# Pooled attention and a top-1 mixture of experts in one kernel: V's columns set in their slots by VectorE products with a mask in PSUM, in place of small DMA copies

## The chip, the cores and the metric

One core of one Trainium2 chip runs the whole kernel. The metric is the device time of one execution in microseconds (us), as the median of several runs.

## What is computed

Eight batches of eight heads, 576 tokens each, 64 wide. Keys and values are averaged over groups of 8 tokens, so that each head has 72 pooled keys. Attention over them gives 4608 tokens of 512 numbers. A gate (512 x 8) sends each token to one of eight experts, and the expert is two matrix products with a relu between.

```python
k_p = k.reshape(B, H, Sp, pool, D).mean(axis=3)
v_p = v.reshape(B, H, Sp, pool, D).mean(axis=3)
scores = scale * np.matmul(q, k_p.transpose(0, 1, 3, 2))
attn = np.exp(scores - np.max(scores, axis=-1, keepdims=True))
attn = attn / (np.sum(attn, axis=-1, keepdims=True) + 1e-09)
x = np.matmul(attn, v_p)
...
logits = x @ w_gate
expert_idx = np.argmax(logits, axis=1)
...
    h = np.maximum(x_sorted[lo:hi] @ w1[e], 0.0)
    y_sorted[lo:hi] = h @ w2[e]
return gate_w[:, None] * y
```

## The kernel before

The order of the work is written out by hand. It has two stages.

**Attention: 36 units.** A unit is 128 tokens of one batch with all eight heads. Batches go in pairs: units 0 to 3 are the first batch of a pair, 4 to 7 the second, and unit 8 takes the last 64 tokens of both; four pairs give 36 units. So batch 2 starts in unit 9, batch 3 in 13, batch 4 in 18, batch 5 in 22, batch 6 in 27 and batch 7 in 31. The loop at L1008 issues for unit i, in this order:

- `u_pt` (L520): TensorE turns the unit's probabilities (`both`) in five pieces of 128 columns into the PSUM tile `pp` (L524); ScalarE copies it to `ph` in fp16 (L526). `pp` has one buffer of 1024 columns, of which 640 are used.
- `g_s` (L485): scores of a later unit into `ps` (L500), `g_qt`: queries turned into `pq` (L477).
- `u_lo` (L529): VectorE makes `pl`, what fp16 lost of `pp` (L532); `g_min` (L507): `nmx`, a minimum over the scores (L510); ScalarE's exponentials follow (L517).
- `u_pv` (L535): 24 products of `ph` and `pl` with the values in `VB` into `po` (L558, in unit 8 of a pair L553). `po` has one buffer.
- `u_nrm` (L575): VectorE reads `po`, takes reciprocals (`ri`, L588, L590) and writes the normalised rows to `both` (L592).

Pieces of other work, "fillers", are put between the steps of `u_nrm` on VectorE: the routing of earlier units to experts (L616 to L755) and the last steps on V.

**The values' slots.** The pooled rows of a batch are 576 (8 heads by 72), cut in five pieces of 128 partitions. A piece holds rows of up to three heads, and a product in L558 takes all of a piece's rows at once; so each head has a slot of its own in `VB` (5 pieces by 3 slots by 78 columns, high and low halves), which holds that head's rows and zeros elsewhere. The finished columns of a batch stand in `vc` (72 columns per piece: 64 of V and 8 of V times the gate). Two ways lead from `vc` to `VB`:

- batches 0 and 1: `masked` (L448), two VectorE products of `vc`, broadcast over the slots, with a 0/1 mask in SBUF (`mk16`), 1080 elements per partition each;
- batches 2 to 7: the last step on V (`low`, L432) puts 12 small DMA copies in the list `moves`, one for each head and piece (8 to 72 partitions of 2 by 72 fp16). SyncE issues them at L1043, at most four at the end of a unit before unit 30 and at most eight after. One copy of a batch's keys within `BD` (L389) goes by the same list.

`VB` has three buffers. That of batches 2 and 5 is used again, after unit 26, for the rows of the first block of tokens (`xg`, L218). `blank` (L284) clears all of this one and sets columns 72 of the others.

SyncE has one queue in program order: it also issues the loads of K, V and queries, the weight loads (L102), the load of the first routed tokens (`early_load`, L929) and the transposes of these (`turn`, L915). What is behind an entry that waits, waits too. GpSimd pools K and V (L327 to L330), sends rows to their experts (L707), and splits the first tokens for the experts (`first_block`, L900, L901). The first products of the experts (`up_early`, L996) stand within units 33 to 35.

**Experts.** From about unit 35 on the kernel runs blocks of 256 tokens through the experts (L989 to L1326).

`prep` (L831) and the lines behind it say in which unit a batch's steps are issued.

Of the kernel before, what the change touches and what calls it, by code (L numbers as in the profile page):

```python
# [13 lines left out]
OP = mybir.AluOpType  # L14
# [18 lines left out]
def kernel(  # L33
# [248 lines left out]
        nc.gpsimd.memset(BD[i], 0.0)  # L282

    def blank(i):  # L284
        nc.gpsimd.memset(VB[i] if i == 2 else VB[i][:, 1, :, :, 72:73], 0.0)
        nc.gpsimd.tensor_tensor(VB[i][:, 0, :, :, 72:73], mk16[:, :, :, None], z16[:, :, :, None], op=OP.add)

    for i in range(3):
# [114 lines left out]
    def five(pm, o, n):  # L403
        return pm[:, o:o + 5 * n].rearrange("p (c x) -> p c x", c=5)
# [12 lines left out]
    def u_dve(b, early=False):  # L417
        pm, vc = KVS["pu", b], KVS["vc", b]
        ut = work.tile([128, 5, 3, E], F32, name="ut", bufs=1)
        u = five(pm, UU, E)  # L420

        def cross():
            nc.vector.tensor_tensor(ut, pm[:, 0:UX].rearrange("p (c s e) -> p c s e", s=3, e=E),
                                    mks[:, :, :, None].to_broadcast([128, 5, 3, E]), op=OP.mult)

        def gather():
            nc.vector.tensor_reduce(u, ut.rearrange("p c s e -> p c e s"), axis=AX.X, op=OP.add)

        def high():
            nc.vector.tensor_scalar(vc[:, 0, :, D:], u, 1.0, None, op0=OP.mult)  # L430

        def low():  # L432
            KVS.pop(("pu", b))
            nc.vector.tensor_tensor(vc[:, 1, :, D:], u, vc[:, 0, :, D:], op=OP.subtract)
            if b > 1:
                KVS.pop(("vc", b))
                for c in range(5):
                    for s in range(*SLOTS[c]):
                        h = HS[c] + s
                        r0, r1 = max(KP * h, 128 * c) - 128 * c, min(KP * h + KP, 128 * c + 128) - 128 * c  # L440
                        moves.append((VB[b % 3][r0:r1, :, c, s, 0:D + E], vc[r0:r1, :, c, :]))

        first = [cross, gather, high, low] if early else [lambda: v_dve(b), cross, gather, high, low]
        if b < 2:
            first += [lambda: masked(b, 0), lambda: masked(b, 1)]
        fillers[0:0] = [(-1, False, f) for f in first]

    def masked(b, s):  # L448
        vc = KVS["vc", b] if s == 0 else KVS.pop(("vc", b))
        nc.vector.tensor_tensor(VB[b][:, s, :, :, 0:D + E], vc[:, s, :, None, :].to_broadcast([128, 5, 3, D + E]),  # L450
                                mk16[:, :, :, None].to_broadcast([128, 5, 3, D + E]), op=OP.mult)

    units = []
    groups = []
# [65 lines left out]
    def u_pt(i):  # L520
        p = pbuf[i % 4]
        pp = psA.tile([128, 1024], F32, name="pp")
        for c in range(5):
            nc.tensor.transpose(pp[:, c * 128:(c + 1) * 128], p[:, c * 128:(c + 1) * 128], ident)  # L524
        ph = work.tile([128, 640], F16, name="ph")
        nc.scalar.activation(ph, pp[:, 0:640], AF.Copy, scale=SP)  # L526
        PP_[i] = (pp, ph)
# [299 lines left out]
    def put(i, pos, f, *a):  # L827
        assert 0 <= i < NU
        hooks.setdefault((i, pos), []).append((f, a))

    def prep(b, k, v, u):  # L831
        put(k[0], "pe" + k[1], k_pe, b)
        put(k[0], "act" + k[1], k_act, b)
        put(v[0], "pe" + v[1], v_pe, b)
        put(v[0], "act" + v[1], v_act, b)
        put(u[0], "pe" + u[1], u_pe, b)
        put(u[0], "act", v_copy, b)
        put(u[0], "dve", u_dve, b)

    put(0, "act2", k_pe, 1)  # L840
    put(0, "act2", k_act, 1)
# [2 lines left out]
    put(2, "pe", u_pe, 1)  # L844
    put(2, "act", v_copy, 1)
    put(2, "dve", u_dve, 1)
    put(1, "sp", load_kv, 3, kf)
    order = [(b, kf if x == 0 else vf) for b in range(B) for x in range(2)]
    for g in range(NPAIR):
# [158 lines left out]
    for i in range(NU):  # L1008
        A, Z = halves.get(2 * i), halves.get(2 * i + 1)
        Y = halves.get(2 * i - 1)  # L1010
        run(i, "q")
        flush(1)
        if i:
            u_pt(i)
        if A:
            g_s(*A)
        if Y:
            g_exp(*Y)
        if i in turns:
            g_qt(*turns[i])  # L1020
        if (i, "pe") not in hooks:
            fill_pe()
        run(i, "pe")
        if i:
            u_lo(i)
        if A:
            g_min(*A)
            fill()
            g_exp(*A)
        fill()  # L1030
        run(i, "act")
        run(i, "dve")
        if i:
            u_pv(i)
        run(i, "pe2")
        if i == 29:
            KVS["late"] = 1
        if len(pend) > 2:
            flush(1)
        fill_pe()  # L1040
        run(i, "sp")
        for _ in range(min(4 if i < 30 else 8, len(moves))):
            nc.sync.dma_start(*moves.pop(0))  # L1043
        if Z:
            g_s(*Z)
        u_nrm(i, (lambda: g_min(*Z)) if Z else None)
        run(i, "act2")
        run(i, "dve2")
        last = routes(i)
        fill(2 if i >= NU - 3 else 1)  # L1050
# [304 lines left out]
```

## Time and profile before

| | us |
|---|---|
| runs | 625.05, 628.80, 632.38 (median 628.80) |
| profiled execution | 626.51 |
| its span, first to last instruction | 623.9 |
| TensorE busy in the span | 574.6 (92%) |
| VectorE, ScalarE, GpSimd busy | 300.7, 291.2, 273.8 |
| mean granted TensorE clock, 1 is full speed | 0.975 |

The profile is one execution on the hardware. PE is TensorE's matmuls, PEld its weight loads, DVE VectorE, ACT ScalarE, POOL GpSimd, SPq the queue of SyncE. "L558" is line 558 of the kernel before. "[1.52 <-DMA vb<-vc]" behind an instruction says that its engine was idle for 1.52 us before it and that the copy from `vc` to `vb` ended that. Tile names are printed in small letters and without the number of the buffer.

### The profile page before, as it was taken

The numbers are of one execution on the slowest core, as the hardware profiler recorded it, in microseconds if no ns is written. First come the engines' busy times: TensorE is split into PE (matmuls) and PEld (weight loads), VectorE is DVE, ScalarE is ACT, GpSimd is POOL, SyncE is SP. The second block draws the span as 40 slices with busy tenths as digits, with TensorE's granted clock in tenths as the row PEclk, the third lists the DMA queues.
The fourth block names the chain that finished last, engine by engine and source line by source line (L and its number), as shares of the span: only waits on it lengthen the run. The fifth ranks groups of instructions, "written<-read, shape, count | busy, mean of one in ns | idle before, by whom it ended". The sixth has DMA issues, their size and how long they took to land.

```text
span 623.9 us, 15851 instructions
## 1 busy us (share of the span) xinstructions
PE 574.6 (92%) x4695; PEld 423.2 (68%) x4696; DVE 300.7 (48%) x613; ACT 291.2 (47%) x648; POOL 273.8 (44%) x524
## 2 busy tenths in 40 slices
PE   6897889799788898998899999999999989999995
PEld 6786779788767375675667667767667666667663
DVE  6567677677667427222782773123722271222122
ACT  2586679789962126223663672122722361222122
POOL 6799588798776543112342223222311232112213
PEclk9799898899979899999999999999999999999998
DMA  8997679879566745974789498343231334321200
GB/s 236 312 294 236 192 223 265 301 233 272 189 203 256 206 128 122 398 203 88 206 279 295 119 310 310 108 105 79 60 73 54 94 75 105 88 49 54 67 17 31
DMA packets 104171, 108.15 MB, mean 173 GB/s; under 512 B 62278, under 2 KB 72518, under 8 KB 104136
## 3 DMA queue, kind: packets, MB, share of 16 engines
q1 hardware_dynamic: 97496, 86.72, 49.3%
q0 software_dynamic: 6640, 20.99, 9.1%
q8 instruction: 19, 0.31, 0.2%
q14 instruction: 16, 0.13, 0.1%
HBM read 72.99 MB, written 23.37 MB: 154 GB/s over the span
## 4 chain that ended last, share of the span: by engine, by line
PE 50%; SPq 1%; issue 1%; ACT 1%; DVE 1%; ACTq 1%; DMA 0%; POOLq 0%; POOL 0%; DVEq 0%
PE po L1073 14%; PE pq L1073 11%; PE ps L998 4%; PE ps L996 4%; PE ps L997 4%; PE pq L996 2%; PE pp L996 2%; PE pp L997 2%; PE pq L997 2%; PE pq L998 2%; PE pp L998 2%; SPq L918 1%; DMA vb<-x_by_expert 0%; ACTq L1212 0%; ACT w L116 0%
## 5 line engine op out<-in xcount | busy, mean ns | idle before, releaser
L1073 PEld LDWEIGHTS <-bd 128*128 128x128 f16 x936 | 91.5, 98 | 109.8 <-issue 5.2
L1242 POOL TENSOR_TENSOR spacer<-ql,iG 1x1 f32<-1x1 f32 x44 | 20.3, 462 | 200.2 <-ACT ql L1238 195.8
L1067 DVE SCALAR_TENSOR_TENSOR bd<-ps,bd 128x512 f16<-128x512 f32 (+1 forms) x44 | 27.6, 630 | 156.8 <-ACT bd L1064 156.2
L517 ACT ACTIVATE both<-ps,nmx 128x72 f32<-128x72 f32 x288 | 68.6, 328 | 14.1 <-DVE nmx L510 13.4
L1073 PE MATMUL po<-w,bd 128*128 128x512 f16 x264 | 58.9, 379 | 0.0
L1073 PE MATMUL po<-kv,bd 128*128 128x512 f16 x264 | 58.8, 379 | 0.0
L1064 ACT ACTIVATE bd<-ps 128x512 f16<-128x512 f32 (+1 forms) x44 | 24.0, 547 | 70.4 <-PE L996 42.2
L1243 POOL DMA_INDIRECT out_dram<-ql,iG x44 | 46.2, 1050 | 21.4 <-issue 20.3
L500 PE MATMUL ps<-bd,qT 128*128 128x144 f32 x256 | 47.9, 314 | 1.7 <-DVE bd L783 0.9
L558 PE MATMUL po<-vb,ph 128*128 128x146 f16 (+2 forms) x384 | 33.2, 233 | 16.4 <-DMA vb<-vc 9.1
L1073 PE MATMUL pq<-kv,bd 128*128 128x512 f16 x216 | 48.1, 379 | 0.0
L1073 PE MATMUL pq<-w,bd 128*128 128x512 f16 x192 | 45.0, 389 | 2.1 <-issue 2.0
L996 PE MATMUL ps<-kv,qt 128*128 128x256 f16 (+1 forms) x176 | 44.9, 263 | 2.1 <-issue 2.1
L998 PE MATMUL ps<-kv,qt 128*128 128x256 f16 (+1 forms) x176 | 44.8, 263 | 2.0 <-DVE qt L118 2.0
L996 PE MATMUL ps<-kv,w 128*128 128x256 f16 (+1 forms) x176 | 43.1, 258 | 2.0 <-ACT kv L116 1.9
L997 PE MATMUL ps<-kv,qt 128*128 128x256 f16 (+1 forms) x176 | 44.9, 263 | 0.0
L998 PE MATMUL ps<-kv,w 128*128 128x256 f16 (+1 forms) x176 | 43.1, 258 | 1.6 <-DVE w L118 1.6
L707 POOL DMA_INDIRECT x_by_expert<-both,rpos x36 | 36.5, 1013 | 15.5 <-issue 6.0
L997 PE MATMUL ps<-kv,w 128*128 128x256 f16 (+1 forms) x176 | 43.1, 258 | 0.0
L1238 ACT ACTIVATE ql<-po,gB 128x512 f32<-128x512 f32 x22 | 15.0, 684 | 57.8 <-PE L996 33.7
L558 PEld LDWEIGHTS <-ph 128*128 128x128 f16 x384 | 26.4, 99 | 21.0 <-DMA vb<-vc 7.9
L996 PEld LDWEIGHTS <-qt 128*128 128x128 f16 x352 | 34.4, 98 | 8.1 <-issue 2.7
(247 smaller groups left out, 1364.7 us busy)
## 6 DMA issues: line engine op xcount, KB each, us to landing
both<-in_moe_w_dram SPq DMA_DIRECT2D x6, 2048.0 KB, 11.4
st<-in_moe_w_dram SPq DMA_DIRECT2D x6, 2048.0 KB, 14.4
vb<-x_by_expert SPq DMA_DIRECT2D x16, 578.0 KB
st<-in_moe_w_dram SPq DMA_DIRECT2D x8, 1024.0 KB
kv<-in_k_dram SPq DMA_DIRECT2D x7, 1024.0 KB
kv<-in_v_dram SPq DMA_DIRECT2D x7, 1024.0 KB
qt<-in_q_dram SPq DMA_DIRECT2D x6, 1024.0 KB
qt<-in_q_dram SPq DMA_DIRECT2D x4, 512.0 KB
```

What stands on the lines that cost most here:

```text
L500: nc.tensor.matmul(ps[:, x * 2 * KP:(x + 1) * 2 * KP], t[:, h, :], BD[b % 3][:, :, h, :], start=True, stop=True)
L517: nc.scalar.activation(p[:, h * KP:(h + 1) * KP], ps[:, x * KP:(x + 1) * KP], AF.Exp, bias=nmx[:, x:x + 1], scale=-1.0)
L558: nc.tensor.matmul(po[:, half, cols], a[:, c * 128:(c + 1) * 128], VB[b % 3][:, y, c, sl, 0:CW], start=st, stop=False, skip_group_check=True)
L707: st = nc.gpsimd.indirect_dma_start(out=xs, out_offset=bass.IndirectOffsetOnAxis(ap=Z["pos"][:, u:u + 1], axis=0), in_=X[:, u, :], in_offs ...
L996: nc.tensor.matmul(dst, wh, xT[:, d, 0:n], start=(d == 0), stop=False)
L997: nc.tensor.matmul(dst, wh, xT[:, DC + d, 0:n], start=False, stop=False)
L998: nc.tensor.matmul(dst, wl, xT[:, d, 0:n], start=False, stop=(d == DC - 1))
L1064: nc.scalar.activation(pair(hT[0], k, n), ups_of(k, n), AF.Relu)
L1067: V.scalar_tensor_tensor(pair(hT[1], k, n), ups_of(k, n), 0.0, pair(hT[0], k, n), op0=OP.max, op1=OP.subtract)
L1073: nc.tensor.matmul(y, hT[x][:, f, 128 * j:128 * j + 128], W2[s][z][:, f, :], start=(half == x == z == f == 0), stop=(half == z == 1 and f ...
L1242: nc.gpsimd.tensor_tensor(spacer[:, 0:1], ys[j][0:1, 0:1], iG[0:1, j:j + 1].bitcast(F32), op=OP.add)
L1243: st = nc.gpsimd.indirect_dma_start(out=out, out_offset=bass.IndirectOffsetOnAxis(ap=iG[:, j:j + 1], axis=0), in_=ys[j], in_offset=None, b ...
```

## The change

`VB` of every batch is now filled by `masked`, and no copy from `vc` to `VB` is left. For batches 1 to 7 the mask is not `mk16` in SBUF but fp32 in 15 of the free columns of `pp`, 640 to 654: in the units named by `put_masked` TensorE multiplies `mk` by the identity into them, right behind the five turns of that unit. The two products of a batch stand before `u_pv` in the program of one unit each (batches 2 to 7: units 6 and 7, 10 and 11, 13 and 14, 19 and 20, 22 and 23, 28 and 29), those of batch 1 both in unit 3. Batch 0 keeps the mask in SBUF. `moves` now holds only the copies within `BD`, and all that stand in the list are issued at the end of each unit. The buffer of batches 2 and 5 is no longer cleared whole.

```diff
     def blank(i):
-        nc.gpsimd.memset(VB[i] if i == 2 else VB[i][:, 1, :, :, 72:73], 0.0)
+        nc.gpsimd.memset(VB[i][:, 1, :, :, 72:73], 0.0)
...
-            if b > 1:
-                KVS.pop(("vc", b))
-                for c in range(5):
-                    for s in range(*SLOTS[c]):
-                        h = HS[c] + s
-                        r0, r1 = max(KP * h, 128 * c) - 128 * c, min(KP * h + KP, 128 * c + 128) - 128 * c
-                        moves.append((VB[b % 3][r0:r1, :, c, s, 0:D + E], vc[r0:r1, :, c, :]))
+            KVS["whole", b] = True
...
-        if b < 2:
+        if b == 0:
             first += [lambda: masked(b, 0), lambda: masked(b, 1)]
...
     def masked(b, s):
+        assert KVS["whole", b]
         vc = KVS["vc", b] if s == 0 else KVS.pop(("vc", b))
-        nc.vector.tensor_tensor(VB[b][:, s, :, :, 0:D + E], vc[:, s, :, None, :].to_broadcast([128, 5, 3, D + E]),
-                                mk16[:, :, :, None].to_broadcast([128, 5, 3, D + E]), op=OP.mult)
+        m = five(KVS["pp"], MK, 3) if b else mk16
+        nc.vector.tensor_tensor(VB[b % 3][:, s, :, :, 0:D + E], vc[:, s, :, None, :].to_broadcast([128, 5, 3, D + E]),
+                                m[:, :, :, None].to_broadcast([128, 5, 3, D + E]), op=OP.mult)
+
+    MK = 640
+    mask_at = set()
...
+        if i in mask_at:
+            KVS["pp"] = pp
+            nc.tensor.matmul(pp[:, MK:MK + 15], ident, mk.rearrange("p c s -> p (c s)"), start=True, stop=True)
...
+    def put_masked(b, *at):
+        for s, i in enumerate(at):
+            mask_at.add(i)
+            put(i, "dve", masked, b, s)
+
...
+        put_masked(b, u[0] + 1, u[0] + 2)
...
+    put_masked(1, 3, 3)
...
-        for _ in range(min(4 if i < 30 else 8, len(moves))):
+        while moves:
             nc.sync.dma_start(*moves.pop(0))
```

**Three places in the order.** In the changed kernel L509, L523, L534, L590, L592 and L594 are L510, L524, L532, L588, L590 and L592 of before.

VectorE in unit 19 before: from the minimum at the end of unit 18 to the normalised rows of unit 19.

```order
L510 TENSOR_REDUCE nmx<-ps 128x4
L532 SCALAR_TENSOR_TENSOR pl<-pp,ph 128x640
L510 TENSOR_REDUCE nmx<-ps 128x4
L715 TENSOR_REDUCE rso<-roh 128x8
L588 TENSOR_SCALAR ri<-po 128x8
L590 RECIPROCAL ri<-ri 128x8
L685 TENSOR_REDUCE res<-rex 128x6
L592 TENSOR_TENSOR both<-po,ri 128x576
```

The same place in the changed kernel; `vb_163` is the buffer of batches 2 and 5.

```order
L509 TENSOR_REDUCE nmx<-ps 128x4
L534 SCALAR_TENSOR_TENSOR pl<-pp,ph 128x640
L509 TENSOR_REDUCE nmx<-ps 128x4
L717 TENSOR_REDUCE rso<-roh 128x8
L446 TENSOR_TENSOR vb_163<-vc,pp 128x15x72
L590 TENSOR_SCALAR ri<-po 128x8
L592 RECIPROCAL ri<-ri 128x8
L687 TENSOR_REDUCE res<-rex 128x6
L594 TENSOR_TENSOR both<-po,ri 128x576
```

Batch 5's first product stands between the minimum and the reading of `po`. It reads `pp`, which unit 20's turns write next.

TensorE at the start of unit 19 in the changed kernel: scores, the five turns, the mask, scores, queries, keys of batch 6.

```order
L499 MATMUL ps<-bd_159,qT 128x144 x2
L523 MATMUL pp<-ident,both 128x128 x5
L526 MATMUL pp<-mk,ident 128x15
L499 MATMUL ps<-bd_160,qT 128x144 x2
L476 MATMUL pq<-ident,qt_155 128x128 x4
L362 MATMUL pq<-ident,kp 64x128 x4
```

The row L526 is new; the others stand as before.

SyncE in units 29 to 31 before: the load of the first routed tokens, the second part of batch 7's copies, the transposes, a weight load.

```order
L929 DMA vb_163<-x_by_expert 128x2x578
L928 UNCONDITIONAL_BRANCH x2
L1043 DMA vb_162<-vc 40x2x72
L1043 DMA vb_162<-vc 32x2x72
L1043 DMA vb_162<-vc 72x2x72
L1043 DMA vb_162<-vc 24x2x72
L1043 DMA vb_162<-vc 48x2x72
L1043 DMA vb_162<-vc 72x2x72
L1043 DMA vb_162<-vc 8x2x72
L1043 DMA vb_162<-vc 64x2x72
L915 DMA_TRANSPOSE kv_130<-bd_160 128x8x128 x2
L102 DMA st_64<-in_moe_w_dram 128x2x1024
```

The same place in the changed kernel, from the last copy within `BD` on.

```order
L1052 DMA bd_159<-bd_159 64x576
L102 DMA st_64<-in_moe_w_dram 128x2x1024
L936 TENSOR_LOAD oki
L936 ISA x2
L937 COMPARE_AND_BRANCH
L938 DMA vb_163<-x_by_expert 128x2x578
L937 UNCONDITIONAL_BRANCH x2
L924 DMA_TRANSPOSE kv_130<-bd_160 128x8x128 x2
L102 DMA st_64<-in_moe_w_dram 128x2x1024
```

The four copies of batch 7 ahead of the load and the eight behind it are gone from the queue.

## Rows read from the trace of the kernel before

**Rows 1.** Busy times by stretch (PE, PEld, DVE, ACT, POOL, clock, DMA share, GB/s)

```profile
45.00:180.00 135.00, 114.48 (x1175) 103.69 (x1174) 94.36 (x263) 108.01 (x341) 110.34 (x134) 0.95 0.76 231
204.00:624.00 420.00, 402.90 (x2960) 268.32 (x2958) 160.91 (x215) 150.95 (x207) 113.18 (x297) 0.99 0.48 138
```

**Rows 2.** Who waited for the copies of L1043: us in all, times

```profile
  PE po L558: 9.1, 8
```

**Rows 3.** Timeline of PE: five of those eight waits (start, us, what)

```profile
74.03 1.03 PE L558 MATMUL po<-vb,ph 128*128 128x219 f16 x8 [1.52 <-DMA vb<-vc]
...
117.73 0.24 PE L558 MATMUL po<-vb,ph 128*128 128x146 f16 x1 [3.11 <-DMA vb<-vc]
...
136.86 0.58 PE L558 MATMUL po<-vb,ph 128*128 128x73 f16 x7 [1.06 <-DMA vb<-vc]
...
176.55 0.34 PE L558 MATMUL po<-vb,ph 128*128 128x219 f16 x1 [1.66 <-DMA vb<-vc]
177.49 0.96 PE L558 MATMUL po<-vb,ph 128*128 128x73 f16 x7 [0.60 <-DMA vb<-vc]
```

**Rows 4.** Busy times by stretch: behind three of the waits, and two undisturbed units

```profile
73.00:78.00 5.00, 3.97 (x25) 3.71 (x26) 2.13 (x8) 0.91 (x5) 4.16 (x6) 0.66 0.99 322
117.00:123.00 6.00, 5.03 (x34) 4.78 (x35) 3.26 (x13) 1.81 (x4) 4.73 (x5) 0.72 0.64 215
176.00:184.00 8.00, 6.85 (x53) 5.71 (x54) 3.16 (x9) 3.66 (x12) 7.74 (x15) 0.57 0.83 214
104.00:112.00 8.00, 8.00 (x101) 7.39 (x99) 5.36 (x12) 7.70 (x29) 7.38 (x11) 1.00 0.99 279
```

**Rows 5.** Timeline of PE: turns that open units 16, 17, 18, 19 and 33

```profile
104.63 0.71 PE L524 MATMUL pp<-ident,both 128*128 128x128 f32 x5
108.45 0.71 PE L524 MATMUL pp<-ident,both 128*128 128x128 f32 x5
111.97 0.71 PE L524 MATMUL pp<-ident,both 128*128 128x128 f32 x5
120.74 1.27 PE L524 MATMUL pp<-ident,both 128*128 128x128 f32 x5
184.93 0.77 PE L524 MATMUL pp<-ident,both 128*128 128x128 f32 x5
```

**Rows 6.** Durations by line, ns min/median/max: products, normalised rows, GpSimd's pooled V

```profile
L450 DVE TENSOR_TENSOR vb<-vc,mk x4: 1274/1674/1906, 23.5 to 45.8; 128x1080 f16<-128x1080 f16 x4
L592 DVE TENSOR_TENSOR both<-po,ri x36: 746/757/760, 29.9 to 196.9; 128x576 f32<-128x576 f32 x36
L330 POOL TENSOR_TENSOR vp<-st x6: 859/861/1786, 44.7 to 142.7; 128x320 f32<-128x320 f32 x6
```

**Rows 7.** Timeline of DVE: units 6, 7, 10, 15, 16 and 18

```profile
60.52 0.17 DVE L588 TENSOR_SCALAR ri<-po 128x8 f32<-128x8 f32 x1 [1.78 <-PE po L558]
65.84 0.17 DVE L588 TENSOR_SCALAR ri<-po 128x8 f32<-128x8 f32 x1 [1.05 <-PE po L558]
81.92 0.17 DVE L588 TENSOR_SCALAR ri<-po 128x8 f32<-128x8 f32 x1 [1.94 <-PE po L558]
104.27 0.17 DVE L588 TENSOR_SCALAR ri<-po 128x8 f32<-128x8 f32 x1 [0.55 <-PE po L558]
106.17 0.82 DVE L532 SCALAR_TENSOR_TENSOR pl<-pp,ph 128x640 f16<-128x640 f32 x1 [0.35 <-ACT ph L526]
118.19 0.20 DVE L434 TENSOR_TENSOR vc<-pq,vc 128x40 f16<-128x40 f32 x1
119.88 0.17 DVE L588 TENSOR_SCALAR ri<-po 128x8 f32<-128x8 f32 x1 [1.49 <-PE po L558]
```

**Rows 8.** Timeline of SPq and POOL: the first routed tokens, their transposes

```profile
168.95 0.01 SPq L929 DMA_DIRECT2D vb<-x_by_expert  x1
172.62 1.04 POOL L900 TENSOR_TENSOR bd<-vb,zf 128x512 f16<-128x512 f32 x1 [3.71 <-DMA vb<-x_by_expert]
176.25 2.75 SPq L915 DMA_TRANSPOSE kv<-bd  x2
```

## The prediction

> **What bounds the kernel now.** I read the busy times by stretch first. From 204 us on TensorE is busy 402.9 of 420 us [rows 1]; the change touches nothing there. From 45 to 180 us, the attention stage, it is busy 114.5 of 135 us with its clock at 0.95 of full speed, and ScalarE (108.0) and GpSimd (110.3) are nearly as busy; VectorE has 94.4 [rows 1]. So the stage is held by no single engine but by hand-overs between engines that are each some 70 to 85% busy, and what a wait costs there must be read from the unit in which it stands.
>
> The question who waited for the copies from `vc` to `VB` comes next: TensorE, eight times, 9.1 us in all [rows 2]. The timeline shows where: at the first products of batches 2, 4, 5 and 7 (and 0.56 us in batch 6), 1.52, 3.11 (+0.24), 1.06 (+0.36) and 1.66 + 0.60 us [rows 3]. An undisturbed unit takes 3.8 us from one opening turn to the next; unit 18 takes 8.8 [rows 5].
>
> A wait costs more than its own time. Behind three of them the clock falls to its lower level, 1.2 GHz, for part of the time; two undisturbed units beside them run at 1.00 [rows 4]. At half speed a share lost in the mean clock is work lost: (1 - 0.66) x 5 = 1.7 us behind the wait at 74 us, 0.28 x 6 = 1.7 at 117.7, 0.43 x 8 = 3.4 at 176.5. **Gross, the copies hold 9.1 + 6.8 = 15.9 us.**
>
> **The change part by part.**
>
> *What goes.* With the 72 copies no wait for them is left. What is late next, wait by wait:
>
> - Unit 9 (1.52 + 1.7): TensorE goes on at once, but behind it VectorE has V's last steps to do and waits little, so of the clock's share I count 0.6: 2.1 us.
> - Unit 18 (3.35 + 1.7): while TensorE stood, VectorE worked through routing and V's last steps up to 118.39 and then waited only 1.49 us for `po` [rows 7]. The next unit's products need `po` emptied, so only 1.5 us of the wait can be won, and the 1.7 us of clock behind it: 3.2.
> - Unit 22: 1.4, of which I take 1.3. Unit 27: 0.56; ScalarE is late with `ph` there, I take 0.3.
> - Unit 31 (2.26 + 3.4): no fillers of V wait there and no new product stands behind it. The next limit is the experts' first products in unit 33, which need the transposed first tokens. Their load is issued at 168.95, GpSimd waits 3.71 us for it, the transposes start at 176.25 [rows 8]; in the queue before, four copies stand ahead of the load and eight behind it. I expect the load some 2 to 3 us sooner and the transposes with it, so that unit 33, which opens at 184.93 [rows 5], opens some 4 us sooner rather than 5.7: 4.0.
>
> Sum: 2.1 + 3.2 + 1.3 + 0.3 + 4.0 = **10.9 us won**, out of 15.9. Below, nothing is won if the next wait ends just as late; above, all 15.9.
>
> *What is added on VectorE.* Twelve products for batches 2 to 7; the two of batch 1 move. The trace has four of the same size with both inputs in SBUF: 1.27 us at the least, 1.91 at the most [rows 6]. None with the mask in PSUM is there. The rows of L592, 576 elements with one input from PSUM, hold within 746 to 760 ns all through [rows 6]; 1080 elements at the same rate, 504 more at 0.96 per ns, give 0.757 + 0.525 = 1.28. I take 1.27, which is also the least of the four, and keep 1.91 as the other end.
>
> The slow ones of the four go with a slow GpSimd: the pooled V of batch 1 took 1.79 us there against 0.86 elsewhere [rows 6]. The Trainium skill (SBUF — State Buffer, section "SBUF: two separate sides") has a rule for this: a VectorE operation with two inputs in SBUF and a GpSimd operation that reads SBUF need the same port pair, and whoever starts first shuts the other out for the whole instruction. By that rule a mask in PSUM frees both, and twelve products are 15.2 us of VectorE; without it up to 22.9. The trace agrees as far as the doubled rows go; no run here yet shows the product with the mask in PSUM.
>
> Where do they fall? Each stands behind `pl` and the minimum, ahead of the reading of `po`, and two others wait for it: the next unit's turns (it reads `pp`, which has one buffer) and, through `ri` and the normalised rows, the next unit's products (`po` too has one). Queued behind it on VectorE are `ri`, the rows, the next minimum and the next `pl`.
>
> - Units 6, 7 and 10: VectorE waits 1.78, 1.05 and 1.94 us for TensorE just there [rows 7]. Unit 7's loses 0.2, the others nothing. Unit 13's lies beside a TensorE that runs at the lower clock: nothing.
> - The other eight (units 11, 14, 19, 20, 22, 23, 28, 29): an undisturbed unit has 0.55 us of waiting before `ri` and 0.35 before the next `pl` [rows 7]. 1.27 - 0.90 = 0.37, some 0.4 each: 3.2 us. In units 19, 20 and 22 routing pieces or V's last steps already fill that slack, so I add 0.5, 0.5 and 0.8.
> - Batch 1's two: before, one stood ahead of `ri` and one behind; now both ahead, shorter, but they hold `pp`. I count nothing (from -1 to +1).
>
> Sum **5.2 us**; the ends are 0, if every one finds cover, and 12 x 1.91 = 22.9, if none does.
>
> *What is added on TensorE.* Thirteen products of 15 columns. Nearest is a turn of 128 columns, 0.14 us each of the 0.71 for five [rows 5]; below, nothing. Half of them stand where TensorE has no slack: 6.5 x 0.14 = **0.9 us**.
>
> *What moves.* SyncE no longer sits behind a copy that waits for `vc`, so loads are issued earlier, and GpSimd may pool earlier. No wait of TensorE for pooled rows stands out, so I count nothing beyond unit 31. The smaller clearing on GpSimd lies at the very start, beside the first loads: nothing.
>
> **Net** 10.9 - 5.2 - 0.9 = 4.8 us. Against the profiled execution's own time, 626.5 (span 623.9 and 2.6 around it), that is 621.7. This execution lies 2.3 us under the median of the runs, 628.8; on the median's scale the forecast is **624.0**, 0.8% faster. About 1% is what a measurement of this kernel can tell from no change, so the forecast lies just inside that bound.
>
> **Rivals.**
>
> *All of it comes back.* The products lie in waits that the page shows or that hand-overs leave, and the whole 15.9 us goes, less 0.9: 628.8 - 15 = 613.8. For it: VectorE is busy 5.36 of 8 us in undisturbed units [rows 4], so there is room for 1.27 us in a unit of 3.8. Against: the room comes in pieces of 0.55 and 0.35, and in unit 18 VectorE itself ends at 118.39.
>
> *Another transfer or engine takes the wait over.* The copy within `BD` still goes by SyncE's queue, behind the loads, and ScalarE is busy 7.7 of 8 us even in undisturbed units [rows 4]. Then a wait ends when it did and the forecast's 4.8 us shrink to about nothing: 628. Against: those copies are issued three units ahead of their use.
>
> *VectorE becomes the bound: slower.* One mechanism: a product between the minimum and `ri` holds both one-buffer tiles, `pp` and `po`, and the hand-over is too tight for any slack to help. The price is 1.27 to 1.91 us for each of twelve, 15 to 23 us, against 10.9 won: 628.8 + 4.4 to + 12 plus 0.9, about 637. It decides from an average of (10.9 - 0.9) / 12 = 0.83 us on the path for each product; I count 0.43. For it: batch 1's products are two of four that the trace shows at 1.7 us or more. Against: [rows 7], three waits that swallow one each.
>
> That the change doesn't do what it says can be left out: without copies no wait for them can remain.
>
> **How the numbers follow.** The forecast's case, some of the gain given back, has 0.62; its own range is 617 to 630, and a little over half of it lies beyond 1%: 0.33 faster, 0.29 within. All comes back: 0.13, faster. The wait taken over: 0.10, within. VectorE bound: 0.15, of which 0.12 slower by over 1% and 0.03 within. So faster 0.46, within 1% 0.42, slower 0.12. The range of 614 to 633 leaves out half of the first rival and most of the last, less than 0.2.
>
> **What would show it right or wrong.** Right: no wait for a copy into `vb` in the profile after; units 18 and 31 shorter by 3 us or more, with the clock near 1.00 behind them; twelve products near 1.27 us whatever GpSimd does; `ri` 0.4 us or more late in units 14, 23 and 29, and TensorE waiting there for VectorE; unit 33 some 4 us earlier against unit 31. Wrong: products at 1.9 us; new TensorE waits of 1 us or more in the product units; or a wait of the same length at unit 31 for the transposes or ScalarE. A time under 617 would mean that I undercounted the cover, one above 633 that the two one-buffer tiles leave no slack.

## The result, and the profile after

The changed kernel takes 620.82 us (median of six runs, 615.92 to 623.24); the kernel before, run beside it, 629.41. The ratio is 0.988, with a 95% interval of 0.984 to 0.992. Two more lots of runs of the same two kernels gave 0.983 (0.979 to 0.987) and 0.986 (0.982 to 0.991). So the change makes the kernel 1.2 to 1.7% faster, some 8 to 10 us. Ratios and intervals compare fast runs alone (a run over 1.5% above the fastest of its kernel counts as slow), so they are not quite the quotients of the medians, and the profiles of shift_one and ahead_of_pl below are of slow runs. The forecast was 624.0 in a range of 614 to 633, with "faster by over 1%" as its likeliest outcome: right in sign and range, too cautious in size.

The profiled execution of the changed kernel took 623.24 us (span 621.3), 3.3 us less than that of before. The attention stage gained far more than these 3.3 us, and two other places gave part of it back. The readings follow in that order.

The busy times of the changed kernel from 45 to 180 us:

```profile
45.00:180.00 135.00, 120.35 (x1298) 108.50 (x1296) 112.81 (x289) 114.44 (x364) 114.51 (x142) 1.00 0.77 242
```

Against [rows 1], TensorE does 5.9 us more work in the same window and its mean granted clock is 1.00 instead of 0.95. VectorE has gone from 94.4 to 112.8 us: it is now as busy as ScalarE and GpSimd.

The rows of the changed kernel for tiles `vb`, the products with the mask in PSUM and the two of batch 0 with the mask in SBUF (ns min/median/max, first and last start):

```profile
L446 DVE TENSOR_TENSOR vb<-vc,pp x14: 1264/1268/1271, 46.0 to 163.0; 128x1080 f16<-128x1080 f16 x14
L446 DVE TENSOR_TENSOR vb<-vc,mk x2: 1303/1838/2374, 23.6 to 26.9; 128x1080 f16<-128x1080 f16 x2
```

The product with its mask in PSUM takes 1.27 us every time; the two with both inputs in SBUF, 1.30 and 2.37.

Who waited for a copy into `vb` has no answer any more. In its place TensorE waits for the products (changed kernel; us in all, times, longest):

```profile
PEld pp L523 <- DVE vb L446: 2.5, 3, 1.6
PE pp L523 <- DVE vb L446: 1.8, 2, 1.4
...
PE po L560 <- DVE vb L446: 2.5, 1, 2.5
```

The first two rows are the same stops seen from the weight load and from the matmul: turns that wait until a product has read the mask in `pp` (1.35 us in unit 4 behind batch 1's two products, 0.49 in unit 23). The third is batch 0 in the start-up.

The turns that open units 1, 18, 19, 20, 31, 33 and 34 of the changed kernel, to set against [rows 5]:

```profile
33.47 0.77 PE L523 MATMUL pp<-ident,both 128*128 128x128 f32 x5
...
110.19 0.71 PE L523 MATMUL pp<-ident,both 128*128 128x128 f32 x5
114.22 0.71 PE L523 MATMUL pp<-ident,both 128*128 128x128 f32 x5
120.37 0.76 PE L523 MATMUL pp<-ident,both 128*128 128x128 f32 x5
...
167.82 0.71 PE L523 MATMUL pp<-ident,both 128*128 128x128 f32 x5
...
176.20 0.76 PE L523 MATMUL pp<-ident,both 128*128 128x128 f32 x5
179.28 0.74 PE L523 MATMUL pp<-ident,both 128*128 128x128 f32 x5
```

Four more opening turns of the kernel before, those of units 1, 20, 31 and 34, on which the comparison rests:

```profile
31.32 0.77 PE L524 MATMUL pp<-ident,both 128*128 128x128 f32 x5
...
125.17 0.71 PE L524 MATMUL pp<-ident,both 128*128 128x128 f32 x5
...
171.98 0.71 PE L524 MATMUL pp<-ident,both 128*128 128x128 f32 x5
...
188.01 0.74 PE L524 MATMUL pp<-ident,both 128*128 128x128 f32 x5
```

Unit 18 took 8.77 us before and takes 4.03 now; unit 19, however, has grown from 4.43 to 6.15. From unit 31 to unit 33 it was 12.95 us and is 8.38.

From unit 1's opening to unit 34's the kernel before took 156.69 us (31.32 to 188.01) and the changed kernel takes 145.81: **10.9 us less**. But unit 1 opens 2.15 us later (start-up), and ScalarE's first relu of the experts on `pp`, 20.9 us behind unit 34's opening before, comes 25.2 us behind it now. These two rows, of before and of the changed kernel, are that relu with its idle time:

```profile
208.89 1.08 ACT L1064 ACTIVATE bd<-pp 128x512 f16<-128x512 f32 x2 [7.34 <-remote]
```

```profile
204.46 1.08 ACT L1073 ACTIVATE bd<-pp 128x512 f16<-128x512 f32 x2 [11.11 <-remote]
```

"Remote" means that the profile has no releaser for the wait. So of the 8.7 us that the changed kernel is ahead when unit 34 opens, 4.4 are left at this relu.

The stretch from unit 1 to unit 34 is the measure that the experiments use below, since it leaves out both places. Read from the opening turns of each profile:

| kernel | unit 1 opens | unit 34 opens | stretch | ratio to before (95%) |
|---|---|---|---|---|
| before, first profile | 31.32 | 188.01 | 156.69 | |
| before, second profile (before_again) | 30.99 | 185.53 | 154.54 | 0.996 (0.991 to 1.001) |
| changed | 33.47 | 179.28 | 145.81 | 0.988 (0.984 to 0.992) |
| changed (again) | 31.96 | 177.86 | 145.90 | 0.983 (0.979 to 0.987) |
| changed (again_two) | 32.98 | 178.78 | 145.80 | 0.986 (0.982 to 0.991) |
| sb_mask | 32.62 | 188.51 | 155.89 | 1.006 (1.002 to 1.010) |
| all_moves | 31.44 | 197.98 | 166.54 | 1.023 (1.020 to 1.026) |
| b0_psum | 32.59 | 178.41 | 145.82 | 0.989 (0.985 to 0.994) |
| no_products | 32.66 | 175.92 | 143.26 | (other work behind it) |
| twice | 34.92 | 195.16 | 160.24 | 1.018 (1.012 to 1.023) |
| shift_one | 35.38 | 184.87 | 149.49 | 0.992 (0.988 to 0.996) |
| late_pads | 32.23 | 178.09 | 145.86 | 0.991 (0.988 to 0.995) |
| ahead_of_pl | 34.72 | 188.13 | 153.41 | 0.995 (0.993 to 0.998) |
| clear_whole | 34.53 | 180.45 | 145.92 | 0.986 (0.981 to 0.992) |

Runs of again, sb_mask, all_moves and b0_psum share one chip (before: 619.0 us there), no_products, twice, shift_one and late_pads another lot (626.4), before_again, again_two and ahead_of_pl a third (629.3), clear_whole a fourth (628.3). Ratios, not times, are to be compared between lots.

The stretch of the changed kernel repeats within 0.12 us in every profile whose attention stage is the same (the three of the changed kernel, b0_psum, late_pads, clear_whole). That of the kernel with copies does not. Units 1 to 5, 16 to 18, 26, 27 and 33, whose program is the same in shift_one and ahead_of_pl, take the same time there to 0.03 us, so the stretches of these two can be compared as well.

### The profile page after: what moved, and what is told of

Its sections match the earlier page's. It is cut to its first block, busy times and chain, and to the rows that moved or that the text cites. A ratio compares the mean times of both kernels' runs of the same rounds, so it can differ in the third digit from the quotient of the medians.

```text
span 621.3 us, 15783 instructions
## 1 busy us (share of the span) xinstructions
PE 573.8 (92%) x4721; PEld 420.5 (68%) x4722; DVE 313.1 (50%) x625; ACT 291.6 (47%) x648; POOL 269.9 (43%) x524
## 5 line engine op out<-in xcount | busy, mean ns | idle before, releaser
L1082 PE MATMUL pq<-w,bd 128*128 128x512 f16 x192 | 46.5, 394 | 4.4 <-issue 3.5
L499 PE MATMUL ps<-bd,qT 128*128 128x144 f32 x256 | 46.2, 305 | 1.6 <-DVE bd L785 0.9
L1005 PE MATMUL ps<-kv,qt 128*128 128x256 f16 (+1 forms) x176 | 45.6, 267 | 2.1 <-issue 2.1
L1007 PE MATMUL ps<-kv,qt 128*128 128x256 f16 (+1 forms) x176 | 45.7, 267 | 2.0 <-DVE qt L118 2.0
L1006 PE MATMUL ps<-kv,qt 128*128 128x256 f16 (+1 forms) x176 | 45.6, 267 | 0.0
L709 POOL DMA_INDIRECT x_by_expert<-both,rpos x36 | 35.4, 985 | 14.7 <-issue 5.9
L1005 PEld LDWEIGHTS <-qt 128*128 128x128 f16 x352 | 34.7, 99 | 8.2 <-issue 2.6
L1007 PEld LDWEIGHTS <-qt 128*128 128x128 f16 x352 | 34.7, 99 | 7.3 <-issue 3.2
L1005 PEld LDWEIGHTS <-w 128*128 128x128 f16 x352 | 34.4, 98 | 6.3 <-ACT kv L116 2.0
```

Of the source, the lines that this page charges most:

```text
L499: nc.tensor.matmul(ps[:, x * 2 * KP:(x + 1) * 2 * KP], t[:, h, :], BD[b % 3][:, :, h, :], start=True, stop=True)
L709: st = nc.gpsimd.indirect_dma_start(out=xs, out_offset=bass.IndirectOffsetOnAxis(ap=Z["pos"][:, u:u + 1], axis=0), in_=X[:, u, :], in_offs ...
L1005: nc.tensor.matmul(dst, wh, xT[:, d, 0:n], start=(d == 0), stop=False)
L1006: nc.tensor.matmul(dst, wh, xT[:, DC + d, 0:n], start=False, stop=False)
L1007: nc.tensor.matmul(dst, wl, xT[:, d, 0:n], start=False, stop=(d == DC - 1))
L1082: nc.tensor.matmul(y, hT[x][:, f, 128 * j:128 * j + 128], W2[s][z][:, f, :], start=(half == x == z == f == 0), stop=(half == z == 1 and f ...
```

## The experiments

### Does the gain repeat? The kernels once more

*again*: the changed kernel, unaltered.

> The changed kernel once more, for a second profile and more times. In the first profile unit 34 opens 8.7 us earlier than before, but the first relu of the experts on ScalarE comes only 4.4 us earlier (204.46 against 208.89), after 11.1 us of idle time with no releaser (7.3 before). Theory A: the length of that idle time changes from execution to execution; then this profile shows another one (between 6 and 12 us) and the times spread over 616 to 623 as the first six did. Theory B: the experts start at a fixed time, when something loaded at a fixed time is there; then the relu starts at 204 to 205 us again, wherever unit 34 opens.

610.68 us (607.01 to 618.60), ratio 0.983. The first relu on `pp`:

```profile
193.01 1.09 ACT L1073 ACTIVATE bd<-pp 128x512 f16<-128x512 f32 x2 [3.24 <-PE pp L1007]
```

The idle time is 3.2 us and ends with TensorE's last first-layer product: the relu starts 15.2 us behind unit 34's opening, not 25.2. Theory B, a fixed time for the start of the experts, falls. Theory A's range, 6 to 12 us of idle time, isn't met either; all four profiles of this chip have 3.2 to 3.3 us (see the start of the experts below).

*before_again* and *again_two*: both kernels in one lot, for two profiles side by side.

> The kernel before, for a second profile beside one of the changed kernel on the same chip. Theory (the attention stage repeats to a few tenths of a microsecond, and the start of the experts does not): 156 to 157.5 us from unit 1's opening to unit 34's, as in the first profile, and ScalarE's idle time before its first relu on pp another than 7.3 us. Rival (the attention stage of before varies too): that stretch differs by over 2 us.

628.65 us. The stretch is 154.54 us, 2.15 less than in the first profile: the rival's bound is just reached, the copies do not land at the same moment every time. TensorE waited less for them (us, times, longest; 9.1 us in eight waits in [rows 2]):

```profile
PE po L558 <- DMA vb<-vc: 6.5, 7, 1.9
```

> The changed kernel a third time, beside the kernel before on the same chip. Theory: 145.9 us from unit 1 to unit 34; the profile's own gain over that of the kernel before on this chip is 10.8 us up to unit 34, plus or minus what the start-up (some 2 us) and the first relu on pp (3.2 us of idle time to 11.1) do in each; the ratio of the medians lies within 0.979 and 0.992. Rival (the gain up to unit 34 is given back behind it in every run): the median's gain stays under 5 us.

620.12 us, ratio 0.986. The stretch is 145.80, so the gain up to unit 34 between these two profiles is 8.7 us, not 10.8 (the part of before that moved). The relu comes 25.5 us behind unit 34 here, against 22.5 in before_again. The gain of the medians, 9 us, lies above the rival's 5.

### Which part of the change does it?

*sb_mask*: no mask in PSUM, and no mask matmul.

```diff
-        m = five(KVS["pp"], MK, 3) if b else mk16
+        m = mk16
...
-        if i in mask_at:
-            KVS["pp"] = pp
-            nc.tensor.matmul(pp[:, MK:MK + 15], ident, mk.rearrange("p c s -> p (c s)"), start=True, stop=True)
```

> All products take the mask from SBUF, no mask matmul is left. Theory (two SBUF inputs are held up by GpSimd): products of 1.27 to 2.4 us with a mean of 1.6 to 1.9 where they were 1.27, GpSimd instructions beside them twice as long, and a time 2 to 5 us above the changed kernel (about 624). Rival (the place of the mask does not matter on the path): the same as the changed kernel or up to 0.9 us less for the mask matmuls, 620 to 621.

624.17 us: 0.6% slower than the kernel before (ratio 1.006), and by the difference of the two ratios (1.006 - 0.983 = 0.023 of 619) some 14 us behind the changed kernel on the same chip (some 10 to 18 by the two intervals); 10 us of that are in the stretch. Both expectations put the loss too low (2 to 5 us, or none). The fourteen products of batches 1 to 7 take 2.0 us in the mean, just over the theory's 1.6 to 1.9. The products, and two of them with the GpSimd instruction beside each:

```profile
L446 DVE TENSOR_TENSOR vb<-vc,mk x16: 1273/1644/3700, 23.4 to 171.8; 128x1080 f16<-128x1080 f16 x16
```

```profile
59.27 2.90 POOL L327 TENSOR_TENSOR st<-kv 128x1280 f32<-128x1280 f32 x1
59.62 3.70 DVE L446 TENSOR_TENSOR vb<-vc,mk 128x1080 f16<-128x1080 f16 x1
...
85.95 2.92 POOL L327 TENSOR_TENSOR st<-kv 128x1280 f32<-128x1280 f32 x1
86.39 3.63 DVE L446 TENSOR_TENSOR vb<-vc,mk 128x1080 f16<-128x1080 f16 x1
```

The product starts 0.35 us (0.44 in the second pair) behind GpSimd's and ends 1.15 us behind its end (63.32 against 62.17; 90.02 against 88.87): it stands still until GpSimd is done and then takes nearly its usual time. In the changed kernel a product beside a GpSimd instruction shows nothing of it:

```profile
59.52 1.55 POOL L329 TENSOR_TENSOR st<-st 128x640 f32<-128x640 f32 x1
59.91 1.27 DVE L446 TENSOR_TENSOR vb<-vc,pp 128x1080 f16<-128x1080 f16 x1
```

That is the rule of the Trainium skill (SBUF — State Buffer, section "SBUF: two separate sides") that the prediction cited: an exclusive lock, held for the whole instruction, and not a slower share. These rows agree: the GpSimd instruction takes 2.90 us beside the product as it does elsewhere, and in these pairs the whole delay falls on the product. So the mask in PSUM is not a detail: without it the products cost as much as the copies in the stretch (155.9 us against 154.5 and 156.7), and the kernel is 0.6% slower.

*all_moves*: the kernel before, with only the limit on copies per unit lifted.

```diff
-        for _ in range(min(4 if i < 30 else 8, len(moves))):
+        while moves:
             nc.sync.dma_start(*moves.pop(0))
```

> The kernel before, with its 72 copies, but all of the list issued at the end of a unit instead of four or eight. Theory (the copies themselves are late: they wait for vc and then for their own landing): TensorE's waits for them stay over 5 us in all, and the time is 626 to 630. Rival (the limit of four a unit made the waits): waits under 2 us, and a time like the changed kernel's, 620 to 623.

633.14 us, 2.3% slower than before. The theory is wrong in both its points, the rival in its time. No wait of TensorE for a copy into `vb` is left in the profile (the theory said over 5 us), units 9 and 31 fall to 4.0 and 4.6 us as in the changed kernel, so it was the limit that made the copies late. But twelve copies in a row hold SyncE's queue for 13 us (some 1.1 us each), and what stands behind them is late instead: queries, V to be pooled, the first tokens' transposes. Rows of all_moves (timelines of SyncE's queue and of TensorE, and who waited):

```profile
91.66 13.16 SPq L1043 DMA_DIRECT2D vb<-vc  x12
...
117.19 1.11 PE L477 MATMUL pq<-ident,qt 128*128 128x128 f32 x4 [6.63 <-DMA qt<-in_q_dram]
...
193.60 0.37 PE L996 MATMUL ps<-kv,w 128*128 128x256 f16 x1 [6.10 <-DMA kv<-bd]
```

```profile
POOL st L327 <- DMA kv<-in_v_dram: 16.0, 3, 7.6
```

Unit 18 takes 13.3 us, unit 25 9.2 and unit 33 11.2. At the two limits tried, the copies are paid either at their landing or in the queue; the change takes away both. A limit in between, or copies issued from another engine's queue, was not tried.

### What does a product cost?

*no_products*: the products and masks of batches 3 to 7 left out.

```diff
-        put_masked(b, u[0] + 1, u[0] + 2)
+        if b < 3:
+            put_masked(b, u[0] + 1, u[0] + 2)
```

> The products and mask matmuls of batches 3 to 7 are left out (10 products; these batches then multiply with the slots of batches 0 to 2, so what the experts get differs and only the attention stage is compared). From unit 1's opening to unit 34's the changed kernel takes 145.9 us (145.8 in the first profile). Theory (the price of the prediction, 5.2 us for twelve products and 0.9 for the mask matmuls): 10 of them cost 4.3 + 0.7 = 5 us, and that stretch falls to about 141. Rival (nearly all find cover): it falls by less than 2 us. Rival (VectorE is the bound, 1.27 us each): by 10 us or more.

Batches 3 to 7 then multiply with what earlier batches left in the slots, so the experts get other rows and the time of the whole, 645.17 us, says nothing here. The stretch is 143.26 us: 2.6 us less than the 145.9 of the changed kernel, so ten products with their masks cost 0.26 us each on the path. The theory (5) is twice too high, the first rival (under 2) a little too low, VectorE as the bound (10 or more) excluded. By unit, the products add 0.37 in unit 11, 0.65 in 13, 0.19 in 14, 0.44 in 20, 0.59 in 22, 0.37 in 23 and 0.67 in 28, and units 25 and 30 give 0.58 of it back. Unit 19 is long with and without them (6.14 and 6.29). What TensorE waits for there, in no_products, is the last of V's steps for batch 5 on VectorE:

```profile
114.64 0.63 PE L476 MATMUL pq<-ident,qt 128*128 128x128 f32 x4 [1.25 <-DVE vc L434]
```

*twice*: every product of batches 2 to 7 done twice.

```diff
             put(i, "dve", masked, b, s)
+            if b > 1:
+                put(i, "dve", masked, b, s)
```

> Each product of batches 2 to 7 is done twice in its place (12 more of 1.27 us, 15.2 us of VectorE). Theory (the slack beside a product is mostly used up by the first one): the second costs 0.8 to 1.27 us each, the stretch from unit 1 to unit 34 grows from 145.9 to 156 to 161, and the time by 10 to 15 us. Rival (cover left): it grows by less than 5 us.

637.04 us, against 626.36 for the kernel before in that lot. The stretch is 160.24 us, 14.4 more than the changed kernel's: 1.20 us for each of twelve. The theory holds: the first product fits into slack, a second one, of 1.27 us, hardly at all. The rows show where (twice, then the changed kernel in again):

```profile
PE pp L523 <- DVE ri L590: 7.8, 7, 1.8
...
PE pp L523 <- DVE vb L446: 5.0, 5, 1.8
```

```profile
PE pp L523 <- DVE vb L446: 1.8, 2, 1.4
PE pp L523 <- DVE ri L590: 1.6, 4, 0.5
```

Both one-buffer tiles are at work: turns that wait until the mask has been read, and turns behind `ri`, the reading of `po`.

### Would another place be better?

*shift_one*: the products of batches 3 to 7 one unit later.

```diff
-        put_masked(b, u[0] + 1, u[0] + 2)
+        put_masked(b, u[0] + 1 + (b > 2), u[0] + 2 + (b > 2))
```

> The products of batches 3 to 7, and their masks, stand one unit later (11 and 12, 14 and 15, 20 and 21, 23 and 24, 29 and 30). Theory (unit 19 is long, 6.15 us, because V's last steps and the product follow each other on VectorE there, and unit 28 too): unit 19 falls to 5 us or less, unit 28 from 5.42 to 4.8, units 20 and 29 grow by 0.4 at most, and the whole gains 1 to 2 us. Rival (a product costs the same in any unit): what units 19 and 28 lose, 20, 21, 29 and 30 gain, and the time is the same within 0.5 us.

Ratio 0.992, stretch 149.49: 3.6 us longer. Both expectations fail. Unit 28 does fall to 4.8, but unit 19 stays at 5.9 (no_products shows the same: V's last steps of batch 5, which before were done while TensorE stood in unit 18, hold it up). The new places are worse: with the product, unit 12 grows from 4.05 to 5.82, unit 24 from 3.67 to 5.78 and unit 30 from 3.36 to 5.53. In these three the product stands right behind VectorE's first routing steps, and the next turns wait for it. The turns that end unit 12 in shift_one:

```profile
92.74 0.74 PE L523 MATMUL pp<-ident,both 128*128 128x128 f32 x5 [1.39 <-DVE vb L446]
```

*ahead_of_pl*: eleven of the twelve products ahead of `pl`.

```diff
         run(i, "pe")
+        run(i, "lo")
         if i:
             u_lo(i)
...
-            put(i, "dve", masked, b, s)
+            put(i, "lo", soonest, b, s, b > 1)
+            put(i, "dve", soonest, b, s, True)
```

(`soonest` issues a product at the first of the two places at which its `vc` is finished.)

> Eleven of the twelve products of batches 2 to 7 stand ahead of pl in their unit, not between the minimum and the reading of po. Theory (a product costs where it holds the reading of po and the next turns): ahead of pl it holds only pl, behind which TensorE has the 12 products of ph, so the stretch from unit 1 to unit 34 falls from 145.9 towards 143.3, what it is without ten of the products. Rival (pl and the minimum are then as late as po was, ScalarE's exponentials with them): 146 to 150 us.

Ratio 0.995, stretch 153.41: the rival is right, and more. `pl` is late, and TensorE waits for it (ahead_of_pl, then again):

```profile
PEld L560 <- DVE pl L534: 10.1, 12, 1.4
PE po L560 <- DVE pl L534: 7.8, 11, 1.3
```

```profile
PEld L560 <- DVE pl L534: 3.7, 8, 0.7
...
PE po L560 <- DVE pl L534: 2.0, 5, 0.5
```

Units 13 and 14 take 7.36 and 5.49 us there. The twelve products of `ph` are 0.94 us and don't cover 1.27.

### The start-up

*b0_psum*: batch 0's second product takes its mask from PSUM too.

```diff
-        m = five(KVS["pp"], MK, 3) if b else mk16
+        m = five(KVS["pp"], MK, 3) if b or s else mk16
...
-    mask_at = set()
+    mask_at = {0}
```

> In the changed kernel the second product of batch 0 takes its mask from PSUM too (a mask matmul behind unit 0's turns). In the first profile it took 2.37 us beside a GpSimd instruction that took 1.65 us, TensorE waited 2.52 us for it, and unit 1 opened at 33.47 (31.32 before). Theory (the collision is real and costs there): 1.27 us, the wait 1.4 us or less, unit 1 about 1.1 us earlier, and a time 1 us below the changed kernel. Rival (unit 1 is late for another reason, the lower clock at 23.5 us): the product is short, but unit 1 opens no earlier and the time is the same.

The collision in the changed kernel's first profile is this:

```profile
26.86 2.37 DVE L446 TENSOR_TENSOR vb<-vc,mk 128x1080 f16<-128x1080 f16 x1
28.17 1.65 POOL L321 TENSOR_TENSOR st<-st 128x256 f32<-128x256 f32 x1
29.29 0.55 PE L560 MATMUL po<-vb,ph 128*128 128x146 f16 x6 [2.52 <-DVE vb L446]
```

In b0_psum that product takes 1.27 us and TensorE waits 1.4 for it, as the theory says; but unit 1 opens at 32.59 (31.96 in again, on the same chip), and the ratio, 0.989, is not below again's 0.983. The rival's reading fits better: most of the delay is not the product.

*clear_whole*: GpSimd's clearing of the whole buffer put back.

```diff
-        nc.gpsimd.memset(VB[i][:, 1, :, :, 72:73], 0.0)
+        nc.gpsimd.memset(VB[i] if i == 2 else VB[i][:, 1, :, :, 72:73], 0.0)
```

> One part of the change undone: GpSimd clears the whole buffer of batches 2 and 5 at the start again (2 us of GpSimd instead of 0.16). In three profiles with that clearing unit 0 takes 8.1 to 8.8 us from its turns to unit 1's, and TensorE's granted clock is 1.00 from 12 to 16 us; in ten profiles without it 9.0 to 11.5 us, and the clock is below 1.00 there in nine of them. Theory (the shorter clearing shifts the start, and costs 0.9 to 3 us there): unit 0 takes 8.8 us or less, the clock from 12 to 16 us is 1.00, and the time is 1 to 2 us below the changed kernel (ratio 0.981 to 0.985). Rival (chance: the moment at which the clock falls is not tied to the program): unit 0 takes 9 us or more, the ratio stays at 0.983 to 0.988.

Unit 0 takes 9.93 us, ratio 0.986. One sign of the theory came, a granted clock of 1.00 from 12 to 16 us, but not the shorter unit 0: by this one profile the shorter clearing is not what makes unit 1 late. What differs further on is the granted clock. Busy times of 20 to 24 us and 24 to 28 us, before, changed and clear_whole:

```profile
20.00:24.00 4.00, 4.00 (x30) 3.87 (x30) 1.80 (x6) 1.86 (x9) 3.69 (x6) 0.63 1.06 329
24.00:28.00 4.00, 2.39 (x26) 2.08 (x24) 3.72 (x5) 2.93 (x11) 3.84 (x5) 1.00 1.11 300
```

```profile
20.00:24.00 4.00, 4.00 (x25) 3.88 (x26) 1.63 (x6) 1.86 (x8) 3.69 (x6) 0.50 1.06 314
24.00:28.00 4.00, 2.76 (x22) 2.64 (x21) 2.91 (x4) 2.98 (x11) 3.84 (x5) 0.87 1.13 299
```

```profile
20.00:24.00 4.00, 4.00 (x22) 3.79 (x22) 1.10 (x3) 1.39 (x7) 3.66 (x4) 0.50 1.08 313
24.00:28.00 4.00, 4.00 (x30) 3.90 (x29) 2.61 (x6) 2.92 (x9) 3.69 (x7) 0.69 1.13 281
```

TensorE is at its lower level (1.2 GHz, 0.50 in these rows) for most or all of 20 to 24 us in all three, and comes back to 1.00 before 24 us in the first, behind it in the others. In all three profiles of kernels with copies it is back by 24 us, in none of eleven with products. TensorE's instructions before 23 us are the same, in the same order, in all fourteen; their start times differ by up to 2 us. No run here says why the moment differs; it stays open.

### The start of the experts

*late_pads*: two of GpSimd's three pad transfers (padding rows behind the tokens of experts 4 to 7) issued later.

```diff
-    def pad_rest():
-        for c in range((n0 + n1) // 2, 4):
+    def pad_rest(c0, c1):
+        for c in range(c0, c1):
...
-        pad_rest()
+        pad_rest(1, 2)
...
     give(1)
+    pad_rest(2, 4)
```

> Two of GpSimd's three pad transfers at the start of the experts (the rows behind experts 4 to 7) are issued only after the first results have been sent. In the changed kernel the first relu on pp came at 204.46 after 11.1 us of idle time in one profile and at 193.01 after 3.2 us in the other, and the times fall into two groups some 6 to 10 us apart. Theory (the long idle time comes from the burst of transfers there, and how often depends on its size): no long one in the profile, and the six times lie closer, at the lower group. Rival (it has nothing to do with these two transfers): two groups as before, the median the same as the changed kernel's.

Ratio 0.991, and the twelve times lie within 619.1 to 624.6: close together, as the theory has it, but no lower than those of the changed kernel. The idle time, 6.6 us, is not gone; it is shorter than in any other profile of the changed kernel that has it, but what is moved comes back further on: the pads wait for the loads of tokens. Relu and moved pad in late_pads:

```profile
198.77 1.09 ACT L1073 ACTIVATE bd<-pp 128x512 f16<-128x512 f32 x2 [6.61 <-remote]
...
215.89 0.97 POOL L1120 DMA_INDIRECT x_by_expert<-zpad,padi  x1 [10.43 <-DMA vb<-x_by_expert]
```

Nothing is won. Over all profiles, the first relu on `pp` comes so long behind unit 34's opening: 15.2 us in each of the four of one chip (again, sb_mask, all_moves, b0_psum, so with copies as with products); elsewhere 20.9 and 22.5 with copies, 20.7 in late_pads and 23.6 to 25.5 in the seven others with products. Where it is long, TensorE has gaps as well. Busy times of the changed kernel's first profile ahead of its relu, then of again, behind its relu, where the DMA engines are as full:

```profile
200.00:202.00 2.00, 1.23 (x4) 0.13 (x2) 0.00 (x0) 0.00 (x0) 1.70 (x3) 1.00 1.15 90
202.00:204.00 2.00, 1.00 (x2) 0.20 (x2) 0.00 (x0) 0.00 (x0) 0.52 (x2) 0.62 1.22 164
```

```profile
196.00:198.00 2.00, 2.00 (x11) 0.88 (x10) 1.90 (x20) 0.00 (x0) 1.57 (x4) 1.00 1.03 176
198.00:200.00 2.00, 2.00 (x11) 0.93 (x10) 0.40 (x5) 0.69 (x1) 1.76 (x4) 1.00 1.29 197
```

The DMA engines are full in both (shares of 1.03 to 1.29), so a full DMA alone does not stop TensorE. Of ScalarE these rows show less: in again its relu at 193.01 us runs at a share of 0.91 (192 to 194 us), in the changed kernel's first profile it stands still at shares of 0.83 to 0.90 (194 to 200 us). What it waits for in the one and not in the other is open.

## Why the prediction was right, and where its sizes were off

**What bounds the kernel.** Right: the waits for the copies and the clock behind them are gone, and the stretch from unit 1 to unit 34 is 10.9 us shorter in the first pair of profiles, 8.7 in the second.

**The copies, 10.9 us won out of 15.9.** Too small for the first profile. Without ten of the products the stretch is 143.3 us against 156.7: the copies were worth some 13.4 there. Against the second profile, 154.5, they were worth 11.3, so that the forecast's size depends on which execution one reads. In the first, unit 9 gave 2.9 (forecast 2.1). Units 18 and 19 together gave 2.9 in no_products (13.20 to 10.31; forecast 3.2): the argument that only part of that wait can be won was right, but the bill stands in unit 19. Units 31 and 32 gave 4.6 (4.0), and the first tokens' load is issued at 161.09, 7.9 us sooner. Unit 22 gave 1.05 (1.3) and unit 27 0.76 (0.3). What the forecast left out are units 13 and 14, in whose slow clock it saw a cover for the product and no gain: they fell by 1.5 without the products, but in the second profile of the kernel before, with its copies, they are already 1.25 shorter. It took one profile for the waits: they were 9.1 us there and 6.5 in the next.

**The products, 5.2 us, and the mask matmuls, 0.9.** Duration right (1.264 to 1.271 us against 1.27). Cost too high: this is the term of the sum that was most off. For the ten products of no_products the forecast's terms are 5.0 us and 0.7 for their masks; measured are 2.6 for both. The eight units that were put at 5.0 cost 2.5. Most of that miss lies where fillers stand, for which an extra was added: units 19, 20 and 22, put at 0.9, 0.9 and 1.2, cost nothing, 0.4 and 0.6, and units 14 and 29, put at 0.4 each, cost 0.2 and nothing. Unit 13, put at nothing, cost 0.65. The step that failed is the addition unit by unit, each product against the slack of its own unit: unit 19 is bound by V's last steps and not by the product, and 0.6 us of what the others cost was made up in units 25 and 30. Batch 1's two, counted as nothing, cost nothing: units 3 and 4 together take 9.85 us against 10.26 before. For one product the slack was there; twice shows that it ends with it.

**What moves, "nothing beyond unit 31", and "from 204 us on the change touches nothing".** The second failed. On the chips on which ScalarE stops before its first relu, the experts start 23.6 to 25.5 us behind unit 34 with products and 20.9 and 22.5 with copies, so 1 to 5 us of the gain is given back there; on the chip where it does not stop, nothing is. That the changed kernel gives more back is seen in nine profiles, two of them with copies; why is not shown.

**The start-up, "nothing".** Failed by 0.5 to 4.4 us: unit 1 opens at 32.0 to 35.4 us in eleven profiles with products, at 31.0 to 31.4 in three with copies. Putting the longer clearing back did not bring it down; the later return of the clock goes with it.

**The net.** -4.8 forecast; -8.7 to -10.9 in the attention stage, part of it given back at the two ends, -8 to -10 by the ratios. The gain was forecast too small and the price too high, and two losses that the forecast did not have paid for part of both. That 624.0 lies only 3.2 us above the measured time is in part luck.

**The rivals.** "All of it comes back" (613.8) was nearer than the forecast in the attention stage of the first pair of profiles (15 and 4.8 against 10.9 us), not in that of the second (8.7). "VectorE becomes the bound" has the right mechanism, and its own threshold of 0.83 us on the path for each product: 0.26 with the mask in PSUM, 1.2 for a second product. In sb_mask its outcome comes, through another wait: VectorE stands still behind GpSimd, and the kernel is 0.6% slower than before.

## What to carry to other kernels

Copies between two tiles of SBUF on a shared queue were paid here either where they land or by what is queued behind them, and the limit that eased the one made the other; a vector instruction of about a microsecond that finds slack in its unit can be cheaper than both. Before putting it there, look at where its operands lie: beside a busy GpSimd, one operand moved from SBUF to PSUM decided here between 1.2 to 1.7% faster and 0.6% slower. Slack is worth one filling: the first product cost 0.26 us, the second at the same place 1.2, and another place in the unit or the next unit cost 4 to 8 us in all.

## What the runs showed of the hardware that was not expected

- A VectorE product with both inputs in SBUF stood still for some 2.4 us behind a GpSimd instruction of 2.9 us: 3.70 us in all against 1.27 with one input in PSUM. The forecast had 1.91 as its upper end.
- ScalarE's idle time at the start of the experts was 3.2 to 3.3 us in all four profiles of one chip, and 6.6 to 11.1 us in the ten others, where the profile names no releaser.
- TensorE's clock returned to its upper level at different moments in the start-up, for the same instructions: before 24 us in three profiles, behind it in eleven.
